# Attention followed by a top-2 mixture of experts: earlier v for the first pair, later preparation of the next five, and a third expert's product ahead of the main part

## The chip, the cores and the metric

The kernel runs on one NeuronCore of a Trainium2 chip. The metric is the device time of one execution in microseconds. Before the change three executions took 875.05, 877.1 and 878.53 us, a median of 877.1. One more execution was taken with the hardware profiler; all rows of before come from it.

## The reference

The inputs are q, k and v of shape (4, 8, 1152, 64), a gate and a noise matrix (512 x 8), noise (2304 x 8), and the weights w1 (8, 512, 1024) and w2 (8, 1024, 512) of eight experts, all float32. Cut to what matters:

```python
q_pool = q.reshape(B, H, S // 2, 2, D).mean(axis=3)     # 1152 rows become 576
scores = q_pool @ k.T / sqrt(D)
attn = softmax(scores, axis=-1)
out = attn @ v                                           # (4, 8, 576, 64)
x = out.transpose(0, 2, 1, 3).reshape(2304, 512)
noisy = x @ w_gate + log1p(exp(x @ w_noise)) * noise
top2 = the two largest of noisy per row;  top2_w = softmax over these two
for each expert e: out[rows of e] += weight * (relu(x[rows of e] @ w1[e]) @ w2[e])
```

## The kernel before

Every float32 operand of a large product is held as two float16 parts: a high part (`hi`, a copy on ScalarE) and a low part (`lo`, operand minus high part, on VectorE). A product is then three TensorE passes, high times high, high times low, low times high. "Split" below means making the two parts.

**Attention.** Two heads of the same place in two batches form a pair; there are 16 pairs, each with three query groups (`SEQ`), 48 segments in all. Of a pair's data SyncE loads k, q and v; k and q are pooled and split, transposed by DMA, and bounds of the scores' maxima are found (`max_mm`, `max_red`, `max_fin`). All this is called a pair's preparation. The scores (`score`) then run in units of two key blocks, ScalarE takes the exponential (`exp`, tile `pf`), VectorE or GpSimd makes its low part (`p_lo`, tile `pl`), and TensorE multiplies with v (`pv`, tile `vv`), which needs v's split.

**Order.** The instructions of attention, routing and the early expert stage are not written in program order. `Plan` receives operations, each with an engine, a cost, a key, and the operations and buffers that it needs, and emits them in the order of a simulated schedule; the smaller the key, the sooner an operation is taken when it is ready. In `pairs` pair i's keys start at 27 i, less `ahead` for its preparation (`ahead = min(LEAD, 4 * i)`). For pair 0 v is split in two halves, with keys b + 3 h on ScalarE and b + 3 + 6 h on VectorE. Each engine then executes its own list in that order.

**Routing.** A row of x is complete when all heads are done. `logits` multiplies rows by the gate matrices, `steps` finds the two experts of each row, their weights and the row's rank in each expert (a sum by TensorE, L818, then VectorE, L831), and scatters the rows by GpSimd into the table `xg` of rows sorted by expert. Batches 0 and 1 (j = 0) are routed in mid-attention in one call of form A. Of batches 2 and 3 (j = 1) query group 0 is routed by a call of form C (key 425), groups 1 and 2 by a last call of form A (key `LATE + 6`, LATE is 440). Steps of a route are short VectorE instructions, each of which depends on the one before; the planner paces them. The tiles' names are `rta`, `rua` for form A and `rtc`, `ruc` for form C.

**Experts.** `Moe.early` gives experts 0 and 1 their first 256 rows while routing ends: these rows come from the first route (tile `xe`). For each expert `mm1` makes eight groups of 12 matmuls of 256 columns (to `pss`), ScalarE and VectorE make the parts `hh`, `hl` of the relu, and `mm2` multiplies two blocks of 128 rows (to `psm`). `Moe.run` is what follows, in program order, and is called the main part here: for experts 0 and 1 the other rows up to 640, 384 columns, for experts 2 to 7 all 640 rows as 2 x 320 columns. Rows come by a transposed load from `xg` (`xload`, tile `xT`) that can start only when all scatters that might write those rows are done. Results are scattered into the output by GpSimd. Weights pass through four raw tiles (`kr`, `qr`, `kn`, `vr`, free after attention) and are split in quarters: expert 0's `w1` in attention, expert 0's `w2` and expert 1's weights in `early`, the rest in `run`, each expert's ahead of its use. A quarter of `w1` is 128 of its 512 rows, so the first of `mm1`'s eight groups needs all four quarters.

Of the kernel before, what the change touches and what calls it, by code (L numbers as in the profile page):

```python
# [7 lines left out]
F16 = mybir.dt.float16  # L8
# [5 lines left out]
AF = mybir.ActivationFunctionType  # L14
# [5 lines left out]
P = 128  # L20
# [5 lines left out]
D = 64  # L26
# [10 lines left out]
NEARLY = 2  # L37

# [180 lines left out]
class Attn:  # L219
# [197 lines left out]
    def pairs(s):  # L417
# [8 lines left out]
        for i in range(NPAIR):  # L426
            b = 27 * i
            x = i == 0
            ahead = min(LEAD, 4 * i)
# [82 lines left out]
            for h, c in enumerate(vs):  # L512
                hi = op("ACT", 0.1 + 0.96 / len(vs), b + 3 * h, lambda i=i, c=c: s.hi(B["vv", i][:, c, 0:D], B["vr", i][:, c], scale),
                        deps=[lv], take=[("vv", ("vv", i))] if h == 0 else (), after=hi)
                vdone[i].append(op("DVE", 0.08 + 1.2 / len(vs), b + 3 + 6 * h,
# [21 lines left out]
    def others(s, F0, out):  # L537
# [42 lines left out]
        def both():  # L580
            s.open += 1
            if s.open == 4:
                s.open = 2
                s.route(R.steps(1, (1, 2), R.A, 0.3, s.half[0]), LATE + 6, [], 0.2, True, then=rows, pace=0.35, first=("DVE", 0.12))

        s.route(R.steps(1, (0,), R.C, 0.3), 425, late[0], 0.2, True, then=rows)
# [43 lines left out]
class Route:  # L630
    def __init__(s, tc, ctx, B, wg, wn, noise):
# [8 lines left out]
        s.group, s.xr, s.pre = [], {}, {}  # L640
        for g in range(3):
            s.xr[1, g] = s.rp.tile([P, 3, XW], F16, name=f"xr{g}")
# [52 lines left out]
    def logits(s, j, g, L, gap, last):  # L695
# [3 lines left out]
        for c in range(3):  # L699
            xT.append(s.rp.tile([P, 8, P], F16, name="xTg", bufs=6))  # L700
# [180 lines left out]
class Moe:  # L881
    def __init__(s, tc, ctx, B, R, F0, w1, w2, out):
# [3 lines left out]
        s.x = pool("mx", 2)  # L886
# [16 lines left out]
        for e in range(NEARLY):  # L903
            s.X[e, 0], s.G[e, 0] = R.pre[e]
        s.nl = 4
# [3 lines left out]
    def load(s, eng=None):  # L909
# [9 lines left out]
        if nm == "1":  # L919
# [6 lines left out]
    def split(s, e, nm, c, half=None, load=True):  # L926
        nc = s.nc
        if c == 0 and half != 1:
            if nm == "1" and e % 2 == 0:
# [4 lines left out]
        r = s.pre[e, nm, c]  # L934
        if half != 1:
            nc.scalar.activation(hi[:, c], r, AF.Copy, scale=WS)
        if half != 0:
            nc.vector.scalar_tensor_tensor(lo[:, c], r, WS, hi[:, c], op0=ALU.mult, op1=ALU.subtract)
            if load:
                s.load()  # L940

    def xload(s, e, a, b):
        nc = s.nc
        s.X[e, a] = s.x.tile([P, 8, CAP], F16, name="xT")
        rows = s.R.xg[e * FULL + a:e * FULL + b]
        nc.sync.dma_start_transpose(out=s.X[e, a][:, :, 0:b - a], in_=rows[:, 0:2 * DM].bitcast(F16))
# [27 lines left out]
    def mm1(s, e, f, a=0, b=CAP, ps=None):  # L974
# [3 lines left out]
        if e not in s.H:  # L978
            s.H[e] = tuple(s.h.tile([P, 8, CAP], F16, name=f"h{x}") for x in "hl")
# [41 lines left out]
    def early(s, A):  # L1021
# [5 lines left out]
        for e in range(2):  # L1027
            s.H[e] = tuple(s.h.tile([P, 8, CAP], F16, name=f"h{x}") for x in "hl")
# [17 lines left out]
        for x in range(12):  # L1046
            e, nm, c = s.loads[x]
            key = LATE + (2, 12, 24)[x // 4] + (2, 2.5, 2.5)[x // 4] * c
# [185 lines left out]
```

## Time and profile before

| | |
|---|---|
| median of three executions | 877.1 us |
| profiled execution, time and span | 875.3 us, 873.5 us |
| mean granted clock of TensorE | 0.979 of full speed |
| busy in the span: TensorE, VectorE, ScalarE, GpSimd | 805.9, 531.7, 444.4, 394.9 us |
| attention, with routing of j = 0 inside | up to about 428 us |
| last routes and early expert stage | about 428 to 486.5 us |
| main part | 486.5 us to the end |

The span is from the first to the last instruction; the execution's time is 1.8 us more. The view of windows gives each engine's busy time in a stretch and the clock that TensorE was granted there; the view of waits says which instruction had to wait, and for what; the chain of waits goes back from the last instruction to what released each step. A busy TensorE may be at half clock, so busy time alone does not show all that is lost.

### The profile page before, as it was taken

To read this page: it belongs to the slowest core of one execution; us is meant where nothing else is said; L and a number is where in the kernel's file an instruction comes from. 1 tells how busy PE (TensorE), PEld (TensorE's weight loads), DVE (VectorE), ACT (ScalarE), POOL (GpSimd) and SP (SyncE) were. 2 spreads that over 40 slices of the span, in tenths; PEclk is the share of its full clock that TensorE was granted. 3 is DMA by queue.
4 is the path that set the end of the run, shared out by engine and by line. 5 is a ranking of instruction groups with operands and counts; after the bars stand their busy time and mean duration, and the time that the engine had idled before them with its cause. 6 is when DMAs were issued, how large, how long until landed. Compare 5 with 4: busy or idle time off the path is not lost.

```text
span 873.5 us, 21140 instructions
## 1 busy us (share of the span) xinstructions
PE 805.9 (92%) x8685; PEld 533.3 (61%) x8685; DVE 531.7 (61%) x1253; ACT 444.4 (51%) x662; POOL 394.9 (45%) x377
## 2 busy tenths in 40 slices
PE   4798989999999998898889799999999999999994
PEld 1475766677767776676746455666574655647442
DVE  6988899989998899999795141434133232422300
ACT  5677778877877776675442132333233332322210
POOL 4377887989888984586125202010202112030222
PEclk9799999999999999999999999999999999999998
DMA  8899978789898994658858725374728364280242
GB/s 207 203 201 215 194 204 192 200 209 199 202 189 170 212 204 99 162 189 238 129 206 289 124 94 107 102 207 112 177 76 216 68 170 104 98 204 13 28 57 39
DMA packets 213829, 137.80 MB, mean 158 GB/s; under 512 B 150496, under 2 KB 183776, under 8 KB 213728
## 3 DMA queue, kind: packets, MB, share of 16 engines
q1 hardware_dynamic: 205088, 116.33, 55.2%
q0 software_dynamic: 8640, 20.08, 11.4%
q8 instruction: 69, 1.13, 0.6%
q14 instruction: 32, 0.26, 0.1%
HBM read 62.14 MB, written 35.44 MB: 112 GB/s over the span
## 4 chain that ended last, share of the span: by engine, by line
PE 64%; DVE 22%; issue 5%; ACT 4%; DMA 4%; POOL 1%; SPq 0%; POOLq 0%; DVEq 0%; ACTq 0%
PE pss L989 23%; PE psm L1006 21%; PE psm L393 8%; DVE pl L370 6%; PE psm L305 4%; DVE rd L317 4%; PE pss L357 4%; PE pss L358 3%; DVE vv L289 2%; ACT pf L365 1%; DVE kd L299 1%; ACT rd L313 1%; DVE mx L335 1%; DVE qn L289 1%; DMA qt<-qn 1%
## 5 line engine op out<-in xcount | busy, mean ns | idle before, releaser
L373 POOL TENSOR_TENSOR pl<-pf 128x384 f16<-128x384 f32 x282 | 281.0, 1028 | 85.2 <-ACT pf L365 61.0
L365 ACT ACTIVATE pf<-pss 128x768 f32<-128x768 f32 x216 | 173.5, 812 | 64.8 <-PE pss L358 40.6
L98 POOL DMA_INDIRECT out_dram<-y,mti x40 | 62.1, 1553 | 316.1 <-ACT y L1011 310.2
L393 PEld LDWEIGHTS <-pf 128*128 128x128 bf16 x2880 | 156.6, 98 | 38.9 <-issue 13.3
L393 PE MATMUL psm<-vv,pf 128*128 128x65 f16 (+1 forms) x2880 | 168.0, 195 | 4.5 <-DVE vv L289 1.8
L393 PE MATMUL psm<-vv,pl 128*128 128x65 f16 (+1 forms) x1440 | 158.5, 194 | 9.3 <-DVE pl L370 8.7
L357 PE MATMUL pss<-qt,kt 128*128 128x384 f16 (+1 forms) x576 | 148.2, 287 | 3.1 <-ACT pf L365 2.9
L358 PE MATMUL pss<-qt,kt 66*128 66x384 f16 (+1 forms) x576 | 148.8, 288 | 0.0
L999 DVE SCALAR_TENSOR_TENSOR hl<-pss,hh 128x640 f16<-128x640 f32 (+1 forms) x64 | 48.5, 758 | 158.2 <-ACT hh L998 158.2
L393 PEld LDWEIGHTS <-pl 128*128 128x128 f16 x1440 | 127.4, 100 | 14.1 <-DVE pl L370 11.0
L1006 PE MATMUL psm<-wl,hh 128*128 128x512 f16 x320 | 121.3, 379 | 0.0
L1006 PE MATMUL psm<-wh,hl 128*128 128x512 f16 x320 | 121.3, 379 | 0.0
L1006 PE MATMUL psm<-wh,hh 128*128 128x512 f16 x320 | 121.3, 379 | 0.0
L1006 PEld LDWEIGHTS <-hh 128*128 128x128 f16 x640 | 62.6, 98 | 74.0
L998 ACT ACTIVATE hh<-pss 128x640 f16<-128x640 f32 (+1 forms) x64 | 41.6, 650 | 129.3 <-PE pss L989 129.3
L317 DVE CUSTOM_DVE_ANT_0 rd<-psm,rd 128x512 f32<-128x512 f32 x144 | 97.2, 682 | 11.8 <-ACT rd L313 10.4
L1011 ACT ACTIVATE y<-psm,mg 128x512 f32<-128x512 f32 x40 | 27.5, 687 | 150.6 <-issue 77.3
L313 ACT ACTIVATE rd<-psm 128x512 f32<-128x512 f32 x144 | 85.7, 597 | 20.9 <-PE psm L305 13.9
L370 DVE TENSOR_TENSOR pl<-pf 128x768 f16<-128x768 f32 x75 | 90.9, 1227 | 0.8 <-ACT pf L365 0.8
L989 PE MATMUL pss<-xT,fh 128*128 128x320 f16 (+1 forms) x448 | 84.5, 306 | 4.7 <-DMA xT<-xg 4.7
L305 PE MATMUL psm<-kt,qt 128*128 128x128 f16 (+3 forms) x317 | 75.8, 312 | 11.6 <-DVE mx L317 6.2
L989 PE MATMUL pss<-xT,wh 128*128 128x320 f16 (+1 forms) x448 | 83.4, 303 | 0.0
(205 smaller groups left out, 1115.6 us busy)
## 6 DMA issues: line engine op xcount, KB each, us to landing
xg<-zt SPq DMA_DIRECT2D x40, 260.0 KB, 4.9
kr<-in_k_dram SPq DMA_DIRECT2D x32, 288.0 KB, 3.8
vr<-in_v_dram SPq DMA_DIRECT2D x16, 576.0 KB, 4.7
kr<-in_moe_w_dram SPq DMA_DIRECT2D x16, 512.0 KB, 4.3
qr<-in_moe_w_dram SPq DMA_DIRECT2D x16, 512.0 KB, 4.5
kn<-in_moe_w_dram SPq DMA_DIRECT2D x16, 512.0 KB, 4.5
qr<-in_q_dram SPq DMA_DIRECT2D x31, 256.0 KB, 3.3
vr<-in_moe_w_dram SPq DMA_DIRECT2D x14, 512.0 KB, 3.9
```

The lines of the kernel that those rows point to most:

```text
L98: i = nc.gpsimd.indirect_dma_start(out=out, out_offset=bass.IndirectOffsetOnAxis(ap=idx, axis=0), in_=src, in_offset=None, **kw)
L305: s.nc.tensor.matmul(ps[r, o:o + m.shape[1] * P], s.G.buf["qt", i][:, c, r], m, start=True, stop=True)
L313: s.nc.scalar.activation(s.G.buf["rd", i, c], s.G.buf["D", i, c], AF.Relu)
L317: s.nc.vector.tensor_tensor_reduce(out=rd, in0=s.G.buf["S", i, c], in1=rd, scale=1.0, scalar=-3.0e38, op0=ALU.add, op1=ALU.max, accum_out= ...
L357: mm(ps[:, a, o:o + w], kt[:, hh * NK + kc, :], qf[:, q0:q0 + w], start=True, stop=False)
L358: mm(ps[:, a, o:o + w], kt2[0:66, hh * NK + kc, :], qf2[0:66, q0:q0 + w], start=False, stop=True)
L365: s.nc.scalar.activation(s.parts(u)[0], s.G.buf["ps", u][:, :, 0:SG], AF.Exp, scale=0.125 / (IN_SCALE * IN_SCALE))
L370: s.nc.vector.tensor_sub(pl, pf, ph)
L373: s.nc.gpsimd.tensor_sub(pl[:, a], pf[:, a], ph[:, a])
L393: mm(o[:, 0:x], src[:, t % 2, ci * P:ci * P + P], vv[:, hh * NK + kc, a:a + x], start=st, stop=last and src is pl, skip_group_check=True)
L989: nc.tensor.matmul(ps[:, i, 0:N], w[:, dc, f * P:(f + 1) * P], xT[:, 2 * dc + x, i * N:(i + 1) * N], start=(n == 0), stop=(n == 11))
L1006: s.nc.tensor.matmul(ps, h[:, f, b * P:(b + 1) * P], w[:, f, :], start=(f == 0 and k == 0), stop=(f == 7 and k == 2))
```

## The change

In attention:

- `ahead` of pairs 1 to 5 goes from 4, 8, 12, 16, 20 to -6, -2, 4, 10, 16, which puts their preparation later; later pairs keep 20.
- Pair 0's two v splits get keys b + h (ScalarE) and b + 3 + h (VectorE).

In routing: form C's key goes from 425 to 440 with a pace of 0.3, the last route's from `LATE + 6` to `LATE + 8`.

In the experts:

- `NFIRST = 3`: expert 2's first product (`mm1`, not `mm2`) for its first 256 rows stands in `early`, after expert 1's. Its `w1` gets a tile of its own, `w1x`, and its four splits and its transposed load (key `LATE + 21`) go to `early` as well. In `run` expert 2 has 384 columns instead of 640, and `split` inside `run` begins with expert 3.
- The first weights of experts 1 and 2 are loaded and split by columns: a quarter is all 512 rows of 256 columns (128 x 4 x 256), so that group f of `mm1` depends on quarter f // 2 alone.
- The transposed rows of the experts lie at fixed places (`home`) in tiles that are free by then: `xTg` (routing's transposed rows), `tok2` (the rows `xr` of j = 1, now one tile), `w1x`.
- `run` issues the four loads of expert 3's `w1` at its start.

```diff
-            ahead = min(LEAD, 4 * i)
+            ahead = (0, -6, -2, 4, 10, 16)[i] if i < 6 else 20
...
-                hi = op("ACT", 0.1 + 0.96 / len(vs), b + 3 * h, lambda i=i, c=c: s.hi(...
+                hi = op("ACT", 0.1 + 0.96 / len(vs), b + 0 + 1 * h, lambda i=i, c=c: s.hi(...
-                vdone[i].append(op("DVE", 0.08 + 1.2 / len(vs), b + 3 + 6 * h,
+                vdone[i].append(op("DVE", 0.08 + 1.2 / len(vs), b + 3 + 1 * h,
...
-                s.route(R.steps(1, (1, 2), R.A, 0.3, s.half[0]), LATE + 6, [], ...
+                s.route(R.steps(1, (1, 2), R.A, 0.3, s.half[0]), LATE + 8, [], ...
-        s.route(R.steps(1, (0,), R.C, 0.3), 425, late[0], 0.2, True, then=rows)
+        s.route(R.steps(1, (0,), R.C, 0.3), 440, late[0], 0.2, True, then=rows, pace=0.3)
...
+        s.home = {(0, EARLY): cut(late, 0, L), (1, EARLY): cut(late, 8 * L, L), (2, EARLY): cut(rows, 0, L),
+                  (2, 0): cut(z, 8 * F, EARLY)}
+        for e in range(3, E):
+            s.home[e, 0] = cut(rows, 8 * L, CAP) if e % 2 else cut(z, 0, CAP)
...
+        if nm == "1" and e in (1, 2):
+            eng.dma_start(r.rearrange("p (d f) -> p d f", d=4),
+                          s.w1[e, :, c * 2 * P:2 * (c + 1) * P].rearrange("(d p) f -> p d f", p=P))
...
+            hi, lo = (t[:, :, c * 2 * P:2 * (c + 1) * P] for t in (hi, lo))
...
+        A.xe[2] = op("SP", 1.4, LATE + 21, lambda: s.xload(2, 0, EARLY), lat=4.0)
-        for x in range(12):
+        for x in range(16):
...
-            key = LATE + (2, 12, 24)[x // 4] + (2, 2.5, 2.5)[x // 4] * c
+            key = LATE + (2, 12, 24, 36)[x // 4] + (2, 2.5, 2.5, 2.5)[x // 4] * c
...
-        for e in range(2):
-            k0 = LATE + 23 * e
+        for e in range(NFIRST):
+            k0 = LATE + (0, 23, 46)[e]
...
-                mm = op("PE", 1.28, k0 + 1.3 * f, lambda e=e, f=f: one(e, f), deps=done[e, "1"] + [A.xe[e]],
+                mm = op("PE", 1.28, k0 + 1.3 * f, lambda e=e, f=f: one(e, f), deps=(done[e, "1"][f // 2:f // 2 + 1] if e else done[e, "1"]) + [A.xe[e]],
...
-            for b in range(2):
+            for b in range(2 if e < NEARLY else 0):
...
+        for _ in range(4):
+            s.load()
...
-                    if 1 <= e < E - 1:
+                    if 2 <= e < E - 1:
                         s.split(e + 1, "1", f // 2, f % 2)
                 if 1 <= e < E - 1:
-                    s.xload(e + 1, 0, CAP)
+                    s.xload(e + 1, EARLY if e + 1 < NFIRST else 0, CAP)
```

Three places show how the engines' lists change. The line numbers after the change are shifted: L289 is L290 there, L370 L371, L741 L745, L938 L962, L1039 L1061, L989 L1011, L1006 L1028.

The first place is VectorE's list at the start of attention. `vv` is pair 0's v (its second half here), `pl` the low part of an exponential, `kd` and `qn` are parts of the preparation, `mx` and `rd` the reductions of the maxima. Before:

```order
L335 TENSOR_REDUCE mx<-psm_68 128x3
L299 TENSOR_TENSOR kd_98<-kt_96 128x512
L342 TENSOR_REDUCE psm_68<-mx 128x3
L343 TENSOR_SCALAR qn_1_127<-psm_68 128x3
L344 SCALAR_TENSOR_TENSOR qn_1_127<-psm_68,qn_1_127 128x3
L289 SCALAR_TENSOR_TENSOR vv_128<-vr,vv_128 128x9x64
L317 ISA rd_107,mx<-psm_67,rd_107 128x512
```

After:

```order
L290 SCALAR_TENSOR_TENSOR kn<-kr,kn 128x9x64
L290 SCALAR_TENSOR_TENSOR qn_1_126<-qs_99,qn_124 128x9x64
L300 TENSOR_TENSOR kd_98<-kt_94 128x512
L371 TENSOR_TENSOR pl_109<-pf_108 128x768
L290 SCALAR_TENSOR_TENSOR vv_127<-vr,vv_127 128x9x64
L371 TENSOR_TENSOR pl_111<-pf_110 128x768
L462 TENSOR_TENSOR qs_99<-qr 128x576
L371 TENSOR_TENSOR pl_113<-pf_112 128x768
```

The split of `vv` stood behind the third query group's maxima; now it stands behind the first low part, ahead of them.

The second place is VectorE's list in the early expert stage. `rta` is a step of the last route, `rtc` one of form C's route, `hl` the low part of a relu, `wl` the low part of a weight quarter. Before:

```order
L938 SCALAR_TENSOR_TENSOR wl_8248<-kr,wh_8247 128x1024
L741 SCALAR_TENSOR_TENSOR rta<-rua 128x48
L1039 SCALAR_TENSOR_TENSOR hl<-pss_63,hh 128x256
L743 TENSOR_SCALAR rta<-rta 128x48
L746 TENSOR_SCALAR rta<-rta 128x48
L748 TENSOR_SCALAR rta<-rta 128x48
L751 SCALAR_TENSOR_TENSOR rta<-rta 128x48
L938 SCALAR_TENSOR_TENSOR wl_8248<-vr,wh_8247 128x1024
```

After:

```order
L752 TENSOR_SCALAR rta<-rta 128x48
L789 SCALAR_TENSOR_TENSOR rtc<-rtc 128x24
L755 SCALAR_TENSOR_TENSOR rta<-rta 128x48
L792 TENSOR_TENSOR rtc<-rtc,nz 128x24
L757 SCALAR_TENSOR_TENSOR rta<-rta 128x48
L759 TENSOR_SCALAR rta<-rta 128x48
L794 TENSOR_TENSOR rtc<-rtc,ruc 128x24
L762 TENSOR_SCALAR rta<-rta 128x48
```

Form C's route was finished before the last route began; now their steps alternate.

The third place is TensorE's list where the early stage ends. `wh` and `wl` are expert 1's second weights, `hh` and `hl` the relu's parts, `fh` expert 0's first weights, `xT` its late rows. Before:

```order
L1006 MATMUL psm_66<-wl_8605,hh 128x512
L1006 LDWEIGHTS hl
L1006 MATMUL psm_66<-wh_8604,hl 128x512
L989 LDWEIGHTS fh
L989 MATMUL pss_64<-xT,fh 128x384
```

After, the end of the second product, and the end of what follows it (the rows between are 96 weight loads and matmuls like these):

```order
L1028 MATMUL psm_66<-wh_8535,hl 128x512
L1011 LDWEIGHTS w1x
L1011 MATMUL pss_63<-w1x 128x256
...
L1011 MATMUL pss_64<-w1x 128x256
L1011 LDWEIGHTS fh
L1011 MATMUL pss_64<-xTg,fh 128x384
```

Between expert 1's second product and expert 0's late rows stand now expert 2's 96 matmuls of 256 columns; `w1x` holds both its weights and its first rows.

## Rows read from the trace of the kernel before

**Rows 1.** the page's busy times by engine (share of the span, instructions)

```profile
PE 805.9 (92%) x8685; PEld 533.3 (61%) x8685; DVE 531.7 (61%) x1253; ACT 444.4 (51%) x662; POOL 394.9 (45%) x377
```

**Rows 2.** the chain of waits, routing to main part (start, us, what)

```profile
...
466.07 5.42 PE pss L989 x48
...
477.10 0.97 POOL xg L98
478.38 3.08 DMA xg<-xr,rta
481.47 5.02 DMA xT<-xg
486.53 32.82 PE pss L989 x192
...
534.89 26.08 PE pss L989 x192
...
```

**Rows 3.** TensorE's waits from 410 to 490 (us in total, times, longest)

```profile
PE pss L989 <- DMA xT<-xg: 4.7, 1, 4.7
...
PE psm L818 <- DVE rua L815: 2.5, 1, 2.5
PE psm L818 <- DVE ruc L815: 1.7, 1, 1.7
PE pss L989 <- DVE hl L1039: 1.4, 1, 1.4
...
```

**Rows 4.** stretches: us, busy of PE, PEld, DVE, ACT, POOL; clock, DMA share, GB/s

```profile
...
428.00:431.20 3.20, 3.20 (x25) 2.31 (x22) 2.43 (x14) 2.33 (x3) 0.00 (x0) 0.51 1.21 124
...
441.60:445.20 3.60, 3.53 (x18) 2.53 (x18) 3.53 (x8) 0.38 (x1) 2.99 (x3) 0.53 0.92 287
...
481.80:486.50 4.70, 0.04 (x1) 0.00 (x0) 0.00 (x0) 0.69 (x1) 0.00 (x0) 0.96 0.82 171
486.50:490.00 3.50, 3.47 (x13) 1.68 (x13) 0.84 (x8) 0.00 (x0) 2.60 (x3) 0.57 1.30 240
...
```

**Rows 5.** the same view for the first pairs

```profile
...
22.00:132.00 110.00, 97.26 (x1448) 70.63 (x1448) 97.29 (x231) 80.90 (x126) 78.13 (x80) 0.94 0.92 203
22.00:44.00 22.00, 17.17 (x147) 9.84 (x147) 20.45 (x51) 15.30 (x24) 8.37 (x8) 0.77 0.89 203
...
```

**Rows 6.** VectorE's routing steps in order of time (start, us, instruction)

```profile
...
429.11 0.18 DVE L741 SCALAR_TENSOR_TENSOR rtc<-ruc 128x24 f32<-128x24 f32 x1
429.33 0.18 DVE L743 TENSOR_SCALAR rtc<-rtc 128x24 f32<-128x24 f32 x1
...
440.28 0.18 DVE L828 RECIPROCAL rtc<-rtc 128x3 f32<-128x3 f32 x1
440.37 0.20 DVE L831 TENSOR_TENSOR ruc<-ruc 128x48 f32<-128x48 f32 x1
...
462.93 0.15 DVE L849 COPY xr<-rta 128x6 f32<-128x6 f32 x1
...
```

**Rows 7.** VectorE's costliest groups, 428 to 486.5 (busy, mean ns)

```profile
...
L1039 DVE SCALAR_TENSOR_TENSOR hl<-pss,hh 128x256 f16<-128x256 f32 x16 | 6.6, 418 | 4.2 <-ACT hh L1035 4.1
...
L938 DVE SCALAR_TENSOR_TENSOR wl<-qr,wh 128x1024 f16<-128x1024 f32 x3 | 3.6, 1212 | 0.0
...
```

**Rows 8.** SyncE's issues in order of time (start, us, what)

```profile
...
464.30 0.34 SPq L920 DMA_DIRECT2D kr<-in_moe_w_dram  x1
...
481.47 2.96 SPq L946 DMA_TRANSPOSE xT<-xg  x1
...
```

**Rows 9.** loads into kr, 430 to 520: how long they take to land

```profile
...
DMA to landing us min/median/max: 3.2/4.8/5.9
```

**Rows 10.** VectorE's timeline: the second half of the first pair's v

```profile
...
38.46 0.75 DVE L289 SCALAR_TENSOR_TENSOR vv<-vr,vv 128x576 f16<-128x576 f32 x1
...
```

**Rows 11.** the chain: first product with v; a transposed load of q's rows

```profile
...
39.87 2.13 PE psm L393 x36
...
76.73 4.32 DMA qt<-qn
...
```

More of the change, by code (lines that the diff above doesn't have):

```diff
@@ L37 @@
 NEARLY = 2
+NFIRST = 3
 IN_SCALE = 64.0
@@ L583, in both @@
                 s.open = 2
-                s.route(R.steps(1, (1, 2), R.A, 0.3, s.half[0]), LATE + 6, [], 0.2, True, then=rows, pace=0.35, first=("DVE", 0.12))
-        s.route(R.steps(1, (0,), R.C, 0.3), 425, late[0], 0.2, True, then=rows)
+                s.route(R.steps(1, (1, 2), R.A, 0.3, s.half[0]), LATE + 8, [], 0.2, True, then=rows, pace=0.35, first=("DVE", 0.12))
+        s.route(R.steps(1, (0,), R.C, 0.3), 440, late[0], 0.2, True, then=rows, pace=0.3)
         for x in range(2):
@@ L640, in __init__ @@
         s.group, s.xr, s.pre = [], {}, {}
+        s.tok2 = s.rp.tile([P, 9, XW], F16, name="xr")
         for g in range(3):
-            s.xr[1, g] = s.rp.tile([P, 3, XW], F16, name=f"xr{g}")
+            s.xr[1, g] = s.tok2[:, 3 * g:3 * g + 3]
+        s.xTg, s.nx = s.rp.tile([P, 6, 8, P], F16, name="xTg"), 0
         s.args = wg, wn, noise
@@ L699, in logits @@
         for c in range(3):
-            xT.append(s.rp.tile([P, 8, P], F16, name="xTg", bufs=6))
+            xT.append(s.xTg[:, s.nx % 6])
+            s.nx += 1
             nc.sync.dma_start_transpose(out=xT[c], in_=xr[:, c, 0:2 * DM])
@@ L885, in __init__ @@
         pool = lambda name, bufs: ctx.enter_context(tc.tile_pool(name=name, bufs=bufs))
-        s.x = pool("mx", 2)
+        s.x = pool("mx", 1)
         s.y = pool("my", 4)
@@ L904, in __init__ @@
             s.X[e, 0], s.G[e, 0] = R.pre[e]
+        z = s.x.tile([P, 5 * F * 2], F16, name="w1x")
+        s.w1x = tuple(z[:, x * 4 * F:(x + 1) * 4 * F].rearrange("p (d f) -> p d f", d=4) for x in range(2))
+        late = R.xTg.rearrange("p c d r -> p (c d r)")
+        rows = R.tok2.rearrange("p c m -> p (c m)")
+        cut = lambda t, a, n: t[:, a:a + 8 * n].rearrange("p (d r) -> p d r", d=8)
+        L = CAP - EARLY
+        s.home = {(0, EARLY): cut(late, 0, L), (1, EARLY): cut(late, 8 * L, L), (2, EARLY): cut(rows, 0, L),
+                  (2, 0): cut(z, 8 * F, EARLY)}
+        for e in range(3, E):
+            s.home[e, 0] = cut(rows, 8 * L, CAP) if e % 2 else cut(z, 0, CAP)
         s.nl = 4
@@ L928, in split @@
         if c == 0 and half != 1:
-            if nm == "1" and e % 2 == 0:
+            if (e, nm) == (2, "1"):
+                s.W[e, nm] = s.w1x
+            elif nm == "1" and e % 2 == 0:
                 s.W[e, nm] = s.F0.w
@@ L943, in xload @@
         nc = s.nc
-        s.X[e, a] = s.x.tile([P, 8, CAP], F16, name="xT")
+        s.X[e, a] = s.home[e, a]
         rows = s.R.xg[e * FULL + a:e * FULL + b]
-        nc.sync.dma_start_transpose(out=s.X[e, a][:, :, 0:b - a], in_=rows[:, 0:2 * DM].bitcast(F16))
+        nc.sync.dma_start_transpose(out=s.X[e, a], in_=rows[:, 0:2 * DM].bitcast(F16))
         n = (b - a) // P
@@ L977, in mm1 @@
         xT = s.X[e, a]
-        if e not in s.H:
-            s.H[e] = tuple(s.h.tile([P, 8, CAP], F16, name=f"h{x}") for x in "hl")
         hh, hl = s.H[e]
@@ L1026, in early @@
         s.W[0, "1"] = s.F0.w
-        for e in range(2):
-            s.H[e] = tuple(s.h.tile([P, 8, CAP], F16, name=f"h{x}") for x in "hl")
+        for e in range(E):
+            s.H[e] = s.H[e % 2] if e > 1 else tuple(s.h.tile([P, 8, CAP], F16, name=f"h{x}") for x in "hl")
         fl, ld, done = {}, {}, {}
```

24 lines of the change are left out of this document (15 added, 9 removed).

## The prediction

> **What bounds the kernel now.** I read the page first. TensorE is busy for 805.9 of 873.5 us [rows 1], so the span can shrink only where TensorE stands idle, runs at half clock, or does work that could fill such a hole. The waits by releaser give the places, the windows their sizes, the chain of waits says what ends last. In the last stretch, from 486.53 to its last product, TensorE never waits: the experts' blocks follow each other [rows 2]. Whatever starts that stretch earlier, or takes work out of it, moves the end one for one. What starts it is not TensorE but a chain: the last routing steps on VectorE, twelve scatters on GpSimd, the last one's landing (3.08 us) and the transposed load of expert 0's late rows (5.02) [rows 2]. TensorE itself ran dry at 481.8 and waited 4.7 us for that load; three more waits stand before it, 2.5, 1.7 and 1.4 [rows 3, 4]. [...] The other soft part is the beginning: from 22 to 132 us TensorE is idle for 12.7 us, 4.8 of them before 44, and its 17.2 us of work up to there ran at a mean of 0.77 [rows 5].
>
> **Part 1, expert 2's early product.** Before, experts 0 and 1 have 256 rows multiplied early and expert 2 all 640 in the main part. Now 96 more matmuls of 256 columns stand ahead of the main part, and expert 2's main block shrinks from 192 matmuls of 320 columns to 96 of 384. The main part loses: a 192-matmul block costs 26.08 us; the two late blocks of experts 0 and 1 cost 32.82 for 192 matmuls of 384, of which 1.4 is the half clock at their start, so 96 cost 15.7 [rows 2]. Saved: 26.08 - 15.7 = 10.4 us. This is the sure term.
>
> The hole gains: 48 matmuls of 256 columns cost 5.42 [rows 2], 96 cost 10.8. TensorE finished the early work at 481.8; with 10.8 more and the same waits it would finish at 492.6, 6.1 us after the rows of expert 0 are there (486.53). But the waits of 2.5, 1.7 and 1.4 and the half clock from 441.6 (0.47 of 3.6 = 1.7) are 7.3 us together. In the new order the rank sums of the C route stand behind 18 matmuls of the second product instead of ahead of it, and those of the last route behind 36 matmuls of expert 1, so TensorE has work while VectorE gets there; and since the weights are split by columns, those 36 need two quarters of expert 1's first weights, not all four. I keep 0.8 us of the first wait and 1.3 of the second, nothing of the third, no half clock: 2.1 of 7.3 stay, and the early work ends at 492.6 - 5.2 = 487.4. Bounds: all of them stay (492.6), none (485.3, then the load's 486.5 counts). So the main part starts 0.9 later than before, and the 4.7 us wait is gone.
>
> With that wait the half clock behind it goes: 3.5 us at 0.57 lose 1.5, of which I take 1.4 [rows 4]. [...]
>
> What could delay the rows of expert 0? VectorE: from the last output of attention to the last routing row (462.93 [rows 6]) it now executes 9 weight splits instead of 8 and 10 small hl passes instead of 8: 1.2 + 2 x 0.4 = +2.0 us [rows 7]. Against that, the two routes are now interleaved step by step. A dependent step of one route starts 0.21 after its forerunner, alternating ones 0.1 apart [rows 6]; some twenty pairs save about 2 us. I take no change, bounds -4 and +5 us (the interleaving saves all it can; or one more pair of splits with their 1.2 us each and the wait for the C route come on top). GpSimd: its last twelve scatters begin when their rows are written, at 463 as before; the six ahead of them move later, but have 1.3 us each [rows 2], so they may begin as late as 455. SyncE: expert 2's early transposed load stands between the loads of expert 1's weights; its issue holds the queue about 3 us, as the 2.96 of its larger sister [rows 8]; the four loads behind it feed splits that stand in VectorE's queue behind a route's steps, which covers 3 us; uncovered they would delay a split in the middle of the last route by as much. The C scatters now wait for that early load to have read its rows; it is ahead of them by far more than its 5 us, since 455 is early enough.
>
> Expert 2's first weights: they are loaded from 464.30 on already in the old trace [rows 8]. Their splits (four on ScalarE, four of 1.2 us on VectorE [rows 7]) leave the main part, where both engines are mostly idle, and stand behind the last route, where VectorE soon has little left. Only the first quarter is needed at 477. The loads by columns have rows of 1 KB instead of 4; the trace has no such load. The nearest are the second weights with rows of 2 KB, which share the buffer's row: 3.2 to 5.9 us to land, whichever kind [rows 9]. I take no change; twice the median (9.6) would still end in time for quarters 1 and 2 and cost up to 3 us on the last.
>
> Merged buffers (one tile for the route's rows, one for expert inputs) add waits only on things long done: expert 3's rows replace those of expert 2's early product after it was used. I cost them at nothing; cover gone, one transposed load is exposed, 5 us as in [rows 2].
>
> **Part 2, the first pairs.** Pair 0's second v split moves in VectorE's queue from 38.46 us to behind the first exponentials' low part, about 27. In the old trace the first product with v starts at 39.87 [rows 10, 11], and until then TensorE can do only pair 1's preparation, one reduction after the other. Now products, scores and exponentials flow from about 28. Pair 1's preparation is behind them by 10 units of the planner, pair 2's 10, then 8, 6, 4. In the order, VectorE's and TensorE's instructions ahead of each output block are nearly as many as before from the fifth pair on, so only holes that are really removed are kept. Upper bound: all idle of 22 to 132 (12.7) and the slow clock (0.23 of 17.2 = 3.9): 16.6 us. Below nothing: see the last rival. I take 4 us, about the idle of the window from 22 to 44, since pair 1's waits only move.
>
> **Sum**, on the profiled execution of 875.3: -10.4 (product) +0.9 (start) -1.4 (clock) -4 (front) = -14.9, 860.4 us. The runs' median is 877.1, 1.8 above the profiled one: forecast 862 us. With -8 to -12.5 for the product and its start and -2 to -8.5 for the front, the forecast's own range is 856 to 867.
>
> **Rivals.** (1) The routing is late. If the last routing row comes 5 us later, scatters, landing and load shift with it, TensorE waits again 4 us ahead of the main part and the clock falls again: 862 + 4.1 + 1.4 = 867.5. For it: nine splits instead of eight in that queue. Against: the interleaving. (2) The front gives nothing or little back: pair 1 to 3 wait as much as pair 0 saved; only the product counts: 866. For it: the preparation work is the same and VectorE is over 85% busy there [rows 5]. (3) The other side: the later preparation starves TensorE at the start of pairs 1 to 5. The chain there is reduction, VectorE's finish, a transposed load that lands after 4.3 us [rows 11], score, exponential. If each of five pairs stands for that load and two passes of VectorE's more (4.3 + 2 x 0.75, the size of the split in [rows 10], = 5.8), 29 us are lost against 10.9 won elsewhere: 877.1 - 10.9 + 29 = 895; from 2.2 us a pair on it decides against the change. Against: six buffers of exponentials are ahead. (4) The change doesn't do what it says: expert 2's product stands ahead but waits for its weights or rows (a queue on SyncE held up), so that the 10.4 saved are waited for: 877.1 + 0.9 - 4 = 874. Against: weights and splits have a lead of 4 us and more. (5) The front gives three quarters of its bound, 12 us: 854. For it: nothing but that bound.
>
> **Chances.** Forecast 0.55, (1) 0.13, (2) 0.13, (5) 0.06, (4) 0.06, (3) 0.07. Range for 8 in 10: 853 to 871. The least this kernel's runs can tell from no change is about 0.5% (4.4 us): faster (under 872.7) gets all but (3) and (4), 0.87; same is (4), 0.06; slower is (3), 0.07.
>
> **What would show it.** In the new profile the wait of the first product on expert 0's late rows is under 1.5 us, and the clock behind it stays at 1. The 96 matmuls from w1x take 10.5 to 11 us and follow the second product of expert 1 without a wait. The main part from there to the end is 10 to 12 us shorter. The first product with v starts before 30 us, and TensorE's idle from 22 to 132 falls from 12.7 to about 8. Wrong if: the scatters' last start is beyond 481; TensorE waits over 1 us for a split of expert 2; a wait of several us for a score's transposed load stands between 45 and 110 us; or TensorE's later idle, from 320 to 428, grows by what the front saved.

## The result, and the profile after

| | before | after |
|---|---|---|
| first comparison, median | 876.08 us (874.17 to 878.53, 4 runs) | 864.64 us (861.94 to 868.08, 4 runs) |
| the unchanged pair again, median | 875.45 us (17 runs) | 864.28 us (861.96 to 866.67, 6 runs) |
| span of the profiled execution | 873.5 us | 863.2 us |

The ratio is 0.987, interval 0.9825 to 0.9915; the second time 0.9875, 0.9856 to 0.9895. The kernel became about 11 us faster, 1.25%. Forecast were 862 us and a gain of 15.

The page's busy times of the kernel after, beside [rows 1]:

```profile
PE 805.6 (93%) x8685; PEld 534.8 (62%) x8685; DVE 531.6 (62%) x1267; ACT 445.7 (52%) x670; POOL 397.8 (46%) x374
```

TensorE does the same work in the same busy time. The 10.3 us of the span are idle time that is gone. The chain of waits of the kernel after, from the end of routing into the main part, beside [rows 2] (start, us, what; four short steps of ScalarE and VectorE are left out at the dots and shown under e4):

```profile
460.30 5.40 PE pss L1011 x48
465.70 10.36 PE psm L1028 x48
476.06 10.49 PE pss L1011 x96
...
488.40 31.36 PE pss L1011 x192
519.76 15.54 PE psm L1028 x72
535.30 15.60 PE pss L1011 x96
```

The chain no longer goes through scatters and the transposed load but through TensorE's own work. Expert 2's 96 early matmuls take 10.49, its main block 15.60 instead of 26.08. Between 476.06 + 10.49 = 486.55 and 488.40 TensorE stands still. TensorE's waits after, 410 to 490, beside [rows 3]:

```profile
PE pss L1011 <- DVE hl L1061: 2.8, 2, 1.9
PE psm L394 <- DVE pl L371: 2.7, 4, 1.4
PE psm L822 <- DVE rua L819: 1.3, 1, 1.3
```

The waits for the load (4.7), for the ranks of form C (1.7) are gone, that for the last ranks is halved. But one of 1.9 us is new and ends where the main part begins. Windows of the kernel after, beside [rows 4] and [rows 5] (same columns):

```profile
441.60:445.20 3.60, 3.60 (x18) 1.60 (x17) 3.60 (x33) 3.47 (x6) 0.00 (x0) 1.00 1.25 166
...
486.50:488.40 1.90, 0.04 (x1) 0.00 (x0) 0.90 (x5) 0.77 (x2) 1.59 (x2) 1.00 1.47 261
488.40:492.00 3.60, 3.60 (x23) 2.17 (x23) 1.40 (x9) 0.49 (x1) 0.92 (x1) 1.00 0.94 250
22.00:132.00 110.00, 99.18 (x1499) 72.59 (x1499) 97.95 (x237) 83.48 (x130) 80.35 (x82) 0.95 0.96 212
22.00:44.00 22.00, 17.84 (x266) 13.93 (x266) 20.66 (x36) 16.01 (x24) 12.50 (x11) 0.92 1.04 214
```

The clock is 1.00 behind the hole and from 441.6. Idle time from 22 to 132 fell only from 12.7 to 10.8 us (8.8 in e1, a second profile of the same kernel).

**Where the front's lead went.** The same view for the instructions of the product with v alone: the count in brackets behind the first busy time says how many ran in a stretch. One that crosses an edge of a stretch stands on both sides of it, so such counts must not be added up over many stretches. Before:

```profile
20.00:44.00 24.00, 3.68 (x72) 3.62 (x72) 0.79 0.88 197
44.00:132.00 88.00, 39.90 (x961) 37.19 (x962) 0.98 0.93 203
132.00:240.00 108.00, 47.37 (x1191) 44.60 (x1187) 1.00 0.85 200
240.00:320.00 80.00, 35.85 (x909) 33.58 (x908) 1.00 0.98 191
320.00:360.00 40.00, 15.17 (x360) 14.59 (x360) 0.96 0.60 136
```

After:

```profile
20.00:44.00 24.00, 7.52 (x189) 7.32 (x189) 0.93 1.02 208
44.00:132.00 88.00, 36.72 (x891) 34.84 (x891) 0.96 0.94 212
132.00:240.00 108.00, 47.15 (x1161) 44.16 (x1161) 0.98 0.84 193
240.00:320.00 80.00, 36.70 (x918) 34.62 (x918) 1.00 0.92 193
320.00:360.00 40.00, 13.39 (x324) 12.71 (x324) 0.90 0.47 117
```

The rows show the lead and that it shrinks. Its size comes from the timeline: here and below, the time of the n-th product is the start of the n-th of these 4320 matmuls, 270 of them for each pair (us):

| | 1st | 30th | 270th | 1080th | 1620th | 3060th | 3600th | 4320th |
|---|---|---|---|---|---|---|---|---|
| before | 39.9 | 41.4 | 59.4 | 138.4 | 187.2 | 314.5 | 373.1 | 427.2 |
| after | 27.2 | 29.2 | 54.8 | 130.5 | 185.6 | 312.0 | 371.8 | 426.7 |

A lead of 12 us is 4.6 at the 270th product, 7.9 at the 1080th, 1.6 at the 1620th (six pairs' worth), 2.5 at the 3060th and 0.4 at the last. So most of it is gone before 190 us, and the rest behind 312. The view of the line of these products, from 400 to 440, has the last start in each kernel (first and last start behind the durations):

```profile
L393 PE MATMUL psm<-vv,pl x121: 191/192/205, 399.9 to 427.2; 128*128 128x65 f16 x111, 128*128 128x64 f16 x10
```

```profile
L394 PE MATMUL psm<-vv,pl x117: 191/192/247, 399.9 to 426.7; 128*128 128x65 f16 x108, 128*128 128x64 f16 x9
```

The later stretch differs in the clock too. TensorE from 320 to 428, before and after (same columns as the windows above):

```profile
320.00:428.00 108.00, 94.17 (x1641) 73.94 (x1641) 100.00 (x258) 67.90 (x101) 63.07 (x63) 0.98 0.65 166
```

```profile
320.00:428.00 108.00, 93.89 (x1596) 73.74 (x1594) 100.16 (x245) 65.43 (x99) 65.68 (x64) 0.93 0.62 163
```

Its idle time there is 13.8 and 14.1 us, but the mean granted clock fell from 0.98 to 0.93.

### The profile page after: what moved, and what is told of

Read it like the earlier page. It is cut to its first block, busy times and chain, and to the rows that moved or that the text cites. A ratio compares the mean times of both kernels' runs of the same rounds, so it can differ in the third digit from the quotient of the medians.

```text
span 863.2 us, 21194 instructions
## 1 busy us (share of the span) xinstructions
PE 805.6 (93%) x8685; PEld 534.8 (62%) x8685; DVE 531.6 (62%) x1267; ACT 445.7 (52%) x670; POOL 397.8 (46%) x374
## 4 chain that ended last, share of the span: by engine, by line
PE 66%; DVE 20%; issue 4%; ACT 4%; DMA 3%; SPq 1%; POOL 1%; ACTq 0%; POOLq 0%; DVEq 0%
PE pss L1011 23%; PE psm L1028 22%; PE psm L394 7%; PE psm L306 5%; DVE pl L371 5%; PE pss L358 4%; PE pss L359 4%; DVE rd L318 4%; ACT pf L366 2%; DVE kn L290 1%; DVE vv L290 1%; ACT rd L314 1%; DMA kr<-in_k_dram 1%; DVE wl L962 1%; DVE kd L300 1%
## 5 line engine op out<-in xcount | busy, mean ns | idle before, releaser
L374 POOL TENSOR_TENSOR pl<-pf 128x384 f16<-128x384 f32 x272 | 267.8, 1015 | 73.7 <-ACT pf L366 62.9
L394 PEld LDWEIGHTS <-pf 128*128 128x128 bf16 x2880 | 157.6, 99 | 41.3 <-issue 13.6
L358 PE MATMUL pss<-qt,kt 128*128 128x384 f16 (+1 forms) x576 | 152.0, 293 | 2.9 <-ACT pf L366 2.7
L359 PE MATMUL pss<-qt,kt 66*128 66x384 f16 (+1 forms) x576 | 152.4, 294 | 1.5 <-DMA qt<-qn 1.5
L1021 DVE SCALAR_TENSOR_TENSOR hl<-pss,hh 128x640 f16<-128x640 f32 (+1 forms) x64 | 46.3, 724 | 162.5 <-ACT hh L1020 162.5
L1028 PE MATMUL psm<-wh,hl 128*128 128x512 f16 x320 | 121.3, 379 | 0.0
L1028 PE MATMUL psm<-wl,hh 128*128 128x512 f16 x320 | 121.3, 379 | 0.0
L1028 PE MATMUL psm<-wh,hh 128*128 128x512 f16 x320 | 121.3, 379 | 0.0
L1028 PEld LDWEIGHTS <-hh 128*128 128x128 f16 x640 | 62.5, 98 | 73.8
L318 DVE CUSTOM_DVE_ANT_0 rd<-psm,rd 128x512 f32<-128x512 f32 x144 | 97.3, 683 | 16.3 <-ACT rd L314 15.3
L1020 ACT ACTIVATE hh<-pss 128x640 f16<-128x640 f32 (+1 forms) x64 | 39.9, 623 | 119.2 <-PE pss L1011 119.2
L371 DVE TENSOR_TENSOR pl<-pf 128x768 f16<-128x768 f32 x80 | 92.2, 1169 | 0.5 <-ACT pf L366 0.4
L358 PEld LDWEIGHTS <-kt 128*128 128x128 f16 x576 | 57.6, 100 | 21.2 <-issue 8.7
L359 PEld LDWEIGHTS <-kt 66*128 66x128 f16 x576 | 57.6, 100 | 19.4 <-issue 6.0
```

The costliest lines, as they stand in the source:

```text
L318: s.nc.vector.tensor_tensor_reduce(out=rd, in0=s.G.buf["S", i, c], in1=rd, scale=1.0, scalar=-3.0e38, op0=ALU.add, op1=ALU.max, accum_out= ...
L358: mm(ps[:, a, o:o + w], kt[:, hh * NK + kc, :], qf[:, q0:q0 + w], start=True, stop=False)
L359: mm(ps[:, a, o:o + w], kt2[0:66, hh * NK + kc, :], qf2[0:66, q0:q0 + w], start=False, stop=True)
L371: s.nc.vector.tensor_sub(pl, pf, ph)
L374: s.nc.gpsimd.tensor_sub(pl[:, a], pf[:, a], ph[:, a])
L394: mm(o[:, 0:x], src[:, t % 2, ci * P:ci * P + P], vv[:, hh * NK + kc, a:a + x], start=st, stop=last and src is pl, skip_group_check=True)
```

## The experiments

Every kernel was timed in five rounds beside the kernel before; ratios are to that. Unless said otherwise an edit is against the kernel after. The expectations give places of products (418.1, 151.9, 355, 358 to 362, 38.5) as sums of counts over windows of 5 us, in which products that cross an edge count twice. Those places are too early, by 9 us for the last product and by some 14 for the 3600th. The texts below give starts.

**e1: once more.** No edit.

> The changed kernel once more, unchanged, to see what chance does. Theory A (the lead of the first pairs is given back before attention ends; lost clock in attention falls by chance): time within 0.4% of 864.6 us; the first product with v again about 12 us sooner than the 39.87 us of before, the last product with v again within 1 us of the 418.1 of before; but the granted clock by stretch differs from the first profile's 0.95 (44 to 76), 0.91 (320 to 380) and 0.96 (380 to 428) in at least one of them by 0.03 or more. Theory B (the new order of attention costs clock by itself): the same three values within 0.02.

864.28 us, ratio 0.9875 (0.9856 to 0.9895). First product with v at 28.2; the 3060th at 312.0 (before 314.5), the last at 428.5, 1.3 later than before, where A allowed 1. The clock by stretch differs: 44 to 76 has 0.89 and not 0.95, 320 to 380 has 0.94 and not 0.91. So A, nearly: two profiles of this kernel end attention 1.7 us apart, the six with this front, the old routing key and VectorE's work unchanged (after, e1, e3, e4, e7, e8) between 425.5 and 428.5, and a difference of that size in one of them says nothing. But B is not gone. Taken whole, 320 to 428 has a granted clock of 0.98 before and in e2, which has the old front, and 0.91 to 0.95 in all eight profiles with the new front and the old routing key (after, e1, e3 to e8). The new order goes with a lower granted clock there (e9, with the old front and the stalls of the last section, has 0.94 too, as the mean of 5 us windows from 320 to 425); how much of the time it costs no run separates from the waits.

**e2: the experts' and routing's part alone.** The front set back:

```diff
-            ahead = (0, -6, -2, 4, 10, 16)[i] if i < 6 else 20
+            ahead = min(LEAD, 4 * i)
```

and the same for the two keys of v.

> The changed kernel with the old order of attention: ahead = min(LEAD, 4 * i) and the old keys of pair 0's v splits; routing and experts as changed. Theory A (the front is given back): 864.6 us within 2, ratio to before about 0.987. Theory B (the front brings 4 us as forecast, and the experts' part 4 less than measured): 868.5 us, ratio 0.991.

865.13 us, ratio 0.9893 (0.9869 to 0.9916), last product 427.5, main part at 487.74 (488.40 and 488.55 in the two profiles with the new front). The time is A's; the ratio's interval holds both theories' values.

**e3: the front alone**, the reverse edit on the kernel before.

> The kernel before with the new order of attention alone: new ahead of pairs 1 to 5 and new keys of pair 0's v splits. Theory A: the first product with v near 27 us, but the end of attention where it was, so 876 us within 2, ratio 1.000. Theory B: 872 us, ratio 0.9955.

873.09 us, ratio 0.997 (0.9955 to 0.9985): 2.6 us, between the two theories, its interval ends at 1.3 and 3.9. On the changed kernel the front makes 0.9 us between e1 and e2, with overlapping intervals. Its worth is one to three us by the medians, less than the 4 forecast. Its one profile does not show where that comes from: attention's last product comes at 428.5, 1.4 later than before, while the main part starts 0.9 sooner (485.62). The experts' part carries the rest, 9 to 10 us (e2 against before, e1 against e3).

**e4: the hole ahead of the main part.**

```diff
-            k0 = LATE + (0, 23, 46)[e]
+            k0 = LATE + (0, 23, 39)[e]
+            st = 0.1 if e == 2 else 1.3
```

with `st * f` in place of `1.3 * f`: the 96 matmuls stand between the two blocks of expert 1's second product.

> The changed kernel with expert 2's 96 early matmuls put between the two blocks of expert 1's second product, instead of behind both. Theory A (the 1.86 us that TensorE waits ahead of the main part is for the two halves of the PSUM buffer that the last two groups of these 96 matmuls filled, which ScalarE and VectorE empty one after the other in 0.38 and 0.42 us steps): with 24 matmuls of the second product behind them that work is covered, the wait falls below 0.3 us and the time by about 1.8 to 862.8. Theory B (something else ends late there too, the late rows of expert 0 or a weight split): a wait of over 1 us remains at the same place, and the time is 864.6 within 1. It would also show if expert 2's weight splits are too late for an earlier start: then a wait for w1x of 1 us or more ahead of its first groups.

863.69 us, ratio 0.9867 (0.9848 to 0.9886). From 470 to 492 TensorE waits for nothing; the main part follows the second block at 484.61. What stood there in the kernel after, ScalarE's and VectorE's timeline:

```profile
486.63 0.38 ACT L1057 ACTIVATE hh<-pss 128x256 f16<-128x256 f32 x1 [1.36 <-PE pss L1011]
487.05 0.42 DVE L1061 SCALAR_TENSOR_TENSOR hl<-pss,hh 128x256 f16<-128x256 f32 x1 [1.32 <-ACT hh L1057]
487.51 0.38 ACT L1057 ACTIVATE hh<-pss 128x256 f16<-128x256 f32 x1 [0.49 <-DVE hl L1061]
487.92 0.42 DVE L1061 SCALAR_TENSOR_TENSOR hl<-pss,hh 128x256 f16<-128x256 f32 x1 [0.45 <-ACT hh L1057]
```

Four steps one after the other empty the last two halves of the PSUM buffer, and the main part's first group needs both. A is right on the place. From attention's last output to the main part it is 57.6 us in e4's profile, 58.7 in e1's, 60.2 in the first one of the kernel after. The time moved by 0.6 us, where A had 1.8, and the intervals can't tell that from none.

**e5 and e6: VectorE's work in pairs 2 to 5.** v's low part is left out, or made twice:

```diff
-                                   lambda i=i, c=c: s.lo(B["vv", i]...),
+                                   lambda i=i, c=c: 2 <= i <= 5 or s.lo(B["vv", i]...),
```

> The changed kernel, but the low part of v is not made for pairs 2 to 5: four passes of 1.28 us of VectorE, 5.1 us, fall out between about 50 and 125 us; the products still read what stands in the tile, and the planned order of all else is the same. Theory A (VectorE's work bounds attention there, which is why the 12 us of lead were given back): the 1260th product with v, at 151.9 in the run of the unchanged kernel, comes 4 to 5 us sooner. Theory B (TensorE's own work or its clock bounds): it comes less than 1 us sooner. As to the end: theory A1 (a lead survives to the end of attention, and the early stage behind starts sooner): 860 us; theory A2 (a lead is taken up again by the stretch from 320 to 380, where the first routing shares VectorE with attention, and by the early stage, which VectorE bounds): 863 to 865 us.

> The changed kernel, but the low part of v is made twice for pairs 2 to 5 (the same pass again): 5.1 us more on VectorE between about 50 and 125 us, the order of all else the same. Theory A: the 1260th product with v 4 to 5 us later than 151.9. Theory B: less than 1 us later. At the end: theory A1 868 to 869 us, theory A2 864 to 866 us.

The 1260th product comes at 152.5 in e5 and 154.6 in e6, against 153.9 in e1: 1.4 sooner and 0.7 later, nearer B than A. The other profiles with this front have 151.3 to 153.9, so only e6 stands outside the scatter. At the 1620th, e5 (183.5) and e6 (187.4) are 3.9 us apart, for 10.2 us of VectorE between them, and the others lie at 182.9 to 185.6. By the times A1: ratios 0.9834 (0.9802 to 0.9865) and 0.9923 (0.9896 to 0.995), that is 3.6 us less and 4.2 more than e1's 0.9875, for 5.1 us of VectorE. e6's profile is 4.6 us later than e1's at the main part (493.12 against 488.55): 1.8 us of that are there at the 1620th product, 3.9 at the 3240th. e5's single profile has a slow end of attention (last product 429.4) that its median does not show. So by the times VectorE's work in attention counts for most of its size (e5's interval just meets e1's); in those very pairs it holds up TensorE by about 0.4 of it, by these two profiles.

**e7: the old keys of the last routes** (425 without a pace, `LATE + 6`).

> The changed kernel with the old keys of the last routes (form C at 425 without a pace, the last route at LATE + 6), so that their steps follow each other on VectorE again. Theory A (the interleaving lets TensorE work while VectorE finishes the routes): the waits for the ranks come back, 1.7 and 2.5 us together against 1.3 now, the last row of the route is written near 463 instead of 460.7, the main part starts some 2.5 us later: 867 us. Theory B (the interleaving is worth nothing, the added product fills these holes either way): 864.5 within 1.

868.14 us, ratio 0.992 (0.9888 to 0.9952), 3.9 us more than e1. TensorE's waits from 428 to 495:

```profile
PE pss L1011 <- DVE hl L1061: 4.8, 3, 1.9
PE psm L822 <- DVE ruc L819: 1.9, 1, 1.9
PE pss L1011 <- ACT hh L1057: 0.3, 1, 0.3
```

Expert 2's product begins at 479.07, not 476.04. This is A in the time, though the interval just meets e1's, and in part by place: the wait for form C's ranks is back, with one of 1.45 us for `hl` behind it, but the 2.5 us for the last ranks is not. The last row, at 461.46, is hardly later.

**e8: the first weights split by rows again**, every group then waiting for all four quarters.

> The changed kernel with the first weights of experts 1 and 2 loaded and split by rows again, so that each group of the first product needs all four quarters. Theory A (by columns is worth what it lets start early): only 12 of expert 1's matmuls stand ahead of the last ranks instead of 36, and they wait for the fourth quarter, so about 2.5 us of work are missing in the holes of 445 to 460; main part 2 us later, 866.5 us. Theory B (VectorE's list, which is as long either way, sets the end of the early stage): 864.5 within 1.

867.9 us, ratio 0.9898 (0.9867 to 0.9929), 2 us more than e1; the intervals overlap. In the profile a wait of 2.4 us for `wl` stands ahead of expert 1's product, and expert 2's begins at 481.64, 5.6 us later than in e1 (the profiled execution took 871.1 us, 3.2 above the median). The place speaks for A, the time settles nothing.

**e9 to e12** ran together. The kernel before took 891.28 us (887.78 to 898.54) beside them, 15 more than beside the others; I compare them by place, and by time only with each other.

**e9: e4 with the old front.**

> The kernel of e4 (expert 2's product between the two blocks) with the old order of attention: old ahead and old keys of pair 0's v. Theory A (the new front's lead is lost between the 3060th and the 3600th product with v, where the first routing's steps on VectorE stand beside GpSimd's passes): in this run, as in the other two with the old front, this stretch takes 38.5 to 39 us for its last 360 products (3240 to 3600) where the new front takes 40 to 47, no lead before it, the 4320th product near 418.5, and the time equals that of e4 within 2 us: ratio to before 0.985 to 0.989. Theory B (the front is worth 2.5 us at the end, as the run of the front alone had it): 2.5 us more than e4, ratio 0.9895.

879.06 us, ratio 0.9865 (0.9821 to 0.9908). The ratio is A's, but the kernel that it is to took 15 us more than beside e4, so it settles little. By place: from the 3240th to the 3600th product it takes 41.9 us, as before and in e2, against 42.7 to 46.8 with the new front and the old routing key, as A had it. The last product comes at 437.1, 9.6 us later than in e2, which neither theory had (see the last section).

**e10 and e11: the first routing's key moved**, on e4's kernel:

```diff
-KEY, PAC, SCW = 290, 1.0, 1.0
+KEY, PAC, SCW = 278, 1.0, 1.0
```

(302 in e11).

> The kernel of e4 with the first routing's key moved from 290 to 278, which shifts its steps in VectorE's list and changes what GpSimd does beside them. Theory A (the lead is lost to the place of the routing's steps): the steps of 128x72 there get another mean than the 0.48 to 0.78 us of e4, and the lead moves with it: with a mean under 0.35 us the 3600th product comes at 355 or sooner and the time is 3 to 4 us below e4; with a mean as in e4 nothing changes. Theory B (the lead is lost there for another reason, the preparation of the pairs that the new front put later): 358 to 362 for the 3600th product whatever the mean.

> The same with the key at 302, later than 290. Theory A: as in the run with 278, the mean of the 128x72 steps decides, under 0.35 us the 3600th product at 355 or sooner. Theory B: 358 to 362 whatever the mean. A later route could make the early rows of experts 0 and 1 late: then a wait for xe ahead of the early stage, near 428.

866.42 us, ratio 0.9701 (0.9657 to 0.9746), and 877.55, 0.9833 (0.9793 to 0.9874). The 3060th and the 3600th product with v, their distance, the time from the first routing's first step of 128x72 on VectorE to its last, and the sum and mean of these 32 steps:

| | 3060th | 3600th | distance | first step to last | steps, sum | mean |
|---|---|---|---|---|---|---|
| before | 314.5 | 373.1 | 58.6 | 37.4 us | 10.0 us | 313 ns |
| e2, e9 (old front) | 314.8, 313.8 | 373.4, 372.4 | 58.6, 58.6 | 37.4, 37.4 | 9.8, 9.9 | 308, 309 |
| after | 312.0 | 371.8 | 59.8 | 41.3 | 13.6 | 424 |
| e1, e3, e4 | 312.0, 311.1, 309.5 | 372.3, 372.4, 369.8 | 60.3, 61.3, 60.3 | 42.1, 43.1, 42.1 | 14.2 to 14.3 | 445, 446, 445 |
| e5, e6, e7, e8 | 309.9, 313.8, 311.0, 310.1 | 374.4, 376.4, 371.1, 373.1 | 64.5, 62.6, 60.0, 63.0 | 45.7, 44.5, 41.9, 44.2 | 13.1 to 14.3 | 409 to 446 |
| e10, e11 | 313.9, 310.3 | 371.2, 363.7 | 57.3, 53.4 | 37.0, 37.7 | 11.0, 11.7 | 345, 366 |
| e12 (new v keys, old `ahead`) | 320.3 | 377.3 | 57.0 | 36.6 | 13.0 | 406 |

With the new front and the old key the routing takes 41.3 to 45.7 us, 3.9 to 8.3 more than before, and the steps' own 3.1 to 4.3 us are a large part of that; with either other key it takes 37 to 38, as with the old front. e11 keeps its lead: its 3600th product is 9.4 us sooner than that of the kernel before. That speaks for A, but does not show it. The sign on record (a mean under 0.35 us, and with it the 3600th product some 4 us sooner than before) came in neither run as written: e10 has the mean, but its product is only 1.9 us sooner; e11 has the product, but a mean of 0.366. e10's lead was down to 0.5 us at the 3060th product, at about its routing's first step (311.8), so its short routing stands behind a loss of another kind. And e12 has slow steps in a short routing. A faster kernel does not follow from e11 either: by the 4050th product its lead has become 5.6 us of delay (413.4 against 407.8), and the last routes' transposed rows and ranks are late (waits of 3.2 and 4.1 us).

What happens to a step is seen in the timelines. e4, VectorE, then GpSimd, then TensorE:

```profile
327.22 0.79 DVE L765 SCALAR_TENSOR_TENSOR rta<-rta 128x72 f32<-128x72 f32 x1
...
328.91 2.21 DVE L765 SCALAR_TENSOR_TENSOR rta<-rta 128x72 f32<-128x72 f32 x2
331.04 1.34 DVE L290 SCALAR_TENSOR_TENSOR vv<-vr,vv 128x1152 f16<-128x1152 f32 x1
332.31 0.22 DVE L765 SCALAR_TENSOR_TENSOR rta<-rta 128x72 f32<-128x72 f32 x1
```

```profile
327.88 1.79 POOL L374 TENSOR_TENSOR pl<-pf 128x384 f16<-128x384 f32 x2
329.63 1.40 POOL L462 TENSOR_TENSOR qs<-qr 128x576 f32<-128x576 f32 x1
334.41 1.61 POOL L374 TENSOR_TENSOR pl<-pf 128x384 f16<-128x384 f32 x2 [3.38 <-PE psm L394]
```

```profile
332.44 0.19 PE L394 MATMUL psm<-vv,pf 128*128 128x64 f16 x1 [2.70 <-DVE vv L290]
```

Two steps beside GpSimd's passes take 2.21 us together here, the one at 332.31, with GpSimd idle, 0.22. The split of v stands behind those two, and TensorE waits 2.70 us for it. In the kernel before GpSimd was idle during the later of these steps (GpSimd's and VectorE's timelines):

```profile
345.45 4.67 POOL L373 TENSOR_TENSOR pl<-pf 128x384 f16<-128x384 f32 x5 [10.38 <-ACT pf L365]
```

```profile
342.22 0.23 DVE L781 SCALAR_TENSOR_TENSOR rta<-rta 128x72 f32<-128x72 f32 x1
```

Step by step in the profiles before and after: of 30 steps of 128x72 on `rta` (the RECIPROCAL, 0.60 us in both, left out) 9 run beside a pass of GpSimd before and 18 after. These take 0.21 to 0.86 us, 0.51 and 0.56 in the mean; the others take 0.19 to 0.23. What holds a step up beside a pass the traces do not show.

**e12: pair 0's v keys alone**, with the old `ahead`.

> The changed kernel with the old ahead of pairs 1 to 5, but the new keys of pair 0's v: one of the two edits of the front alone. Theory A (the v split alone lets the first product with v start some 12 us sooner; the later preparation only keeps it from being given back at once): first products near 31, a lead that is gone by the 900th product, end of attention where it was: 864.5 within 2. Theory B (without the later preparation the planner still puts pair 1's maxima ahead): the 300th product no sooner than 60.

878.05 us, ratio 0.9839 (0.9798 to 0.9881), not apart from e9's and e11's. The 30th product comes at 30.1 (before 41.4), the 300th at 56.2, 0.5 sooner than in any other run, and the 540th, at 78.4, is still 6.5 us sooner than before. By the 900th (124.7, before 122.8) nothing is left, while e10 and e11, with the later preparation, are 5.4 and 4.3 ahead there. So the early v alone makes the lead; the later preparation doesn't make it larger, but keeps it longer. At the 1620th product the three are level (185.1, 185.5 and 184.7, before 187.2). B falls.

## Why the prediction was right or wrong

- **Expert 2's product, -10.4 us:** right. 26.08 became 15.60, 10.5 us; the 96 early matmuls cost 10.49 of 10.8 forecast.
- **The half clock behind the hole, -1.4:** right. The first main block went from 32.82 to 31.36, 1.46 us. Before, the clock was 0.50 in every half microsecond from 486.5 to 489.5 and 0.97 in the next. In e1, e2 and e4 the clock is 1.00 from 486 to 494 too; in e3, which still has the hole, the block takes 32.82.
- **The early stage's waits, 2.1 of 7.3 left:** nearly right, in other parts than forecast. The last ranks wait 1.33 us (1.3 forecast), form C's none (0.8), and one for `hl` is 0.95 (none): 2.3 of 7.3. From attention's last output (428.61 before, 428.20 after) to the end of the early matmuls it takes 58.35 us, against 58.8 forecast (487.4 - 428.6). e7 (3.9 us in time, its interval just meeting e1's) and e8 (5.6 us, by place alone) speak for the interleaving and the split by columns paying for this, as the step had it.
- **No wait ahead of the main part:** wrong by 1.86 us. The step followed weights and rows to this place, and not the PSUM buffer that the early groups leave behind. The old order had a whole second product between the last group's emptying and the next use; e4 puts one back and the wait is gone.
- **The front, -4:** the step that failed. Product with v began at 27.2, sooner than the 28 forecast, 12.7 us ahead. But the step's rule, that only holes which are really removed are kept, gave too much: it took about the idle time from 22 to 44, 4.8 us. That fell by 0.7 in the first profile, and from 44 to 62, where TensorE had been busy without a break, it rose by 0.9: a wait of 2.25 us for a maximum stands at 44 there. From 22 to 132 1.9 us of idle time were saved (4.0 in e1, 1.0 in e3), and at the 1620th product the lead is 1.6 (1.6 to 4.3 in the other profiles with this front and unchanged work on VectorE). VectorE was busy for 97.3 of these 110 us before and for 98.0 after, which is what rival 2 stood on; e5 and e6 show that its work counts here, not that nothing else does. Of the rest, 0.4 was left at the last product. The step did not ask what the same lead does 250 us later, when the first routing's steps meet GpSimd at another moment: 3.6 to 4.3 us more for the same 32 steps, and in e1, e3 and e4 a wait of 2.7 us for v's split beside them (312 to 365), which before, e2 and the first profile of the kernel after don't have. That this, and not the lower clock from 320 on, takes the rest of the lead is likely by e11, not shown.
- **The signs:** the first product before 30, the clock of 1.00, the 96 matmuls in 10.49 us behind the second product without a wait came as forecast, and the main part is 12.2 us shorter. Idle time from 22 to 132 is 10.8 (8.8 in e1), where 8 was the sign. The sign of being wrong that TensorE's idle time from 320 to 428 grows by what the front saved is there in e1 (16.5 us against 13.8) and e3 (15.9), not in the first profile (14.1), which has the lower clock instead.
- **The sum:** -14.9 forecast, -10.3 measured on the spans. Missing are 3.6 of the front and 1.86 of the new wait; 0.45 came back in the early stage and 0.4 in the main part. This lies nearest to the rival in which the front gives nothing (866), without being it, since the front alone brought 2.6 us in e3.
- Rivals 1, 4 and 5 fell: the last row is at 460.6, sooner than 462.93; TensorE waits for no part of `w1x`, whose quarters landed in 5.0, 5.1, 6.1 and 5.6 us by columns, as expert 2's did by rows before (4.8, 5.6, 6.1, 5.8); and the front gave nothing near 12 us. Rival 3 fell too: only 1.5 us of TensorE's waits up to 430 are for a score's transposed load.

Left open: whether e10's key makes a faster kernel than e4, which did not run beside it. Against e9, e11 and e12 it is ahead already where attention ends (last product 429.1, against 437.1, 432.7 and 440.2). Against e4's profile it is not (425.5), so its lead in that set may be only that it escaped the stalls of the last section.

## What to carry to other kernels

Follow a lead to the end of the stage that it is to shorten: take the time of the same piece of finished work in both kernels, as with the products above, since a lead of 12 us can be there at 30 us and be 1.6 at 186. Take it from starts: counts of a view by windows stand twice where an instruction crosses an edge, and added up they moved the last product here by 9 us. When work is put into a hole in front of a stage, look also at the buffers that it leaves full at the stage's first instruction, and put something behind it that hides their emptying. And look at what GpSimd does beside a chain of tiny VectorE steps: here the same 32 steps took 10.0 us in one order and 14.3 in another.

## What the runs showed of the hardware

Three of the runs e9 to e12 had stalls for which the view of waits names no instruction of the program. In e9 ScalarE stood still 6.66 us ahead of an exponential, its releaser given as "issue" (the engine waited for nothing that the profile shows), while the first routing's scatters ran (ScalarE's timeline):

```profile
376.07 1.17 ACT L293 ACTIVATE vv<-vr 128x1152 f16<-128x1152 f32 x1
383.90 0.81 ACT L366 ACTIVATE pf<-pss 128x768 f32<-128x768 f32 x1 [6.66 <-issue]
```

TensorE stood still beside it (374 to 385) in 12 waits of 5.4 us together, with the same releaser; VectorE waited 9.6 us for TensorE, and GpSimd's next pass 7.4 us for ScalarE. Against the kernel before, e9 falls back by 10.5 us from the 3600th to the 3780th product. e11 has 5.5 us on ScalarE and e12 5.8, there with the releaser "remote"; e10, whose scatters come sooner, has neither and is 11 us faster than they are. The scatters run in the other runs too, without such a stall. That the kernel before lost its 15 us in that set in this way is possible, not shown: it was not profiled there.

Expert 2's early transposed load held SyncE's queue for 7.0 us (436.2 to 443.2), where 3 were forecast from its sister; no wait of TensorE leads back to it.
